# Windowed attention and a squared-ReLU layer on one core: the value products of the later visits by chunk, in quarters of the matmul array

## The chip, the cores and the metric

The kernel runs on one core of a Trainium2 chip. The metric is the device time of one execution in microseconds; a kernel's number is the median of several runs. One execution was profiled besides: its rows are what the prediction reads. A core has five engines that work side by side, each in its own order: TensorE (PE, matmuls), VectorE (DVE), ScalarE (ACT), GpSimd (POOL), and SyncE (SP), which here issues nearly all DMA transfers. PE's rows come in two kinds: PE are the matmuls, PEld the loads of their stationary operand, which lie beside earlier matmuls.

## The reference

```python
for c in range(768 // 32):                       # chunks of 32 queries, 4 batches, 8 heads, 64 wide
    q_c = q[:, :, 32*c : 32*c + 32]
    keys = 8 memory keys + keys from 16 before the chunk to 8 after it
    a = softmax(q_c @ keys.T / 8)
    out[chunk] = a @ values
x = out as 3072 tokens x 512
h = relu(x @ w_in)                               # 512 -> 2048
y = (s * h*h + b) @ w_out                        # 2048 -> 512
```

All is float32. The two large products are done in three matmuls each of a faster 32-bit type, with operands split in a high and a low part.

## The kernel before, in words

The attention is done in blocks of 64 queries (two chunks) against 96 keys: 80 of the block's own window, 16 before and 8 after it counted in, and the rest memory keys with padding. The keys stand in an order such that the first chunk needs keys 0 to 63 and the second keys 32 to 95 (SPANS); the others of the 96 are masked, so that their weights are zero. A visit (attend, L506 on) handles six blocks of a pair of heads, or three blocks of two pairs of heads. There are 32 visits. The first 8 (alone) serve the first 768 tokens; the 24 from the ninth on serve tokens 768 to 1151 (4 visits) and the remaining 1920 tokens (20 visits, whose results go through DRAM, tiles xs, to the later stages).

A visit has these steps. The scores (product, L540): for each of three pairs of blocks and each head four matmuls of 64 x 64 (head width x queries) over 96 keys; a head uses 64 rows of the array, a block 64 of its columns, and the scores of each head of the pair go to a PSUM bank of their own (scs). DVE adds the mask and finds the maximum (L621), ACT takes the exponential and its sum (L625), POOL multiplies by the reciprocal of the sum (L637). The weights are transposed to keys x queries (tile aT): by PE for the first 8 visits, by 32 x 32 blocks on DVE from the ninth on (flip, L654). Then come the values (value, L581): for each block and head one matmul of 96 keys x 64 columns over 64 queries, into a third bank (va, ring "v"). A float32 matmul of the program is two matmul records and two weight loads in the trace, so the 12 value matmuls of a visit are 24 records, and the 12 score matmuls 24 records as well. ACT copies the sums out (L590 for the 20 visits that go through DRAM; L600, with a subtraction on DVE at L601, for the others).

From the ninth visit on the values of a visit are held back by DEPTH = 2 visits and issued by PE as one operation with the scores of the visit two later:

```python
def both():
    for j in range(last[5] if last else 0):
        last[2](j)          # the held-back visit's values
    for j in range(nj):
        product(j)          # this visit's scores
```

So 22 of the 24 visits have values and scores together, the first two of them scores alone, and at the end two visits' values remain, which are issued by themselves.

The order of all instructions on each engine is fixed beforehand by a planner (Plan.lay, L258): a list scheduler with a hold time per kind of operation (HOLD, SCORES, VALUES), priorities with a table of hand-tuned shifts (NUDGE), and a model of DMA landings. PSUM banks are handed out by the planner too: eight banks, with limits per kind in room (L420): two for scores ("s"), at most three of scores and values together, two for the hidden layer ("h"), three accumulators ("acc"), five for the products of the later stage ("p"). On the chip the engines wait for one another by semaphores, and follow that order.

After the attention of the first 1152 tokens the hidden layer (hidden, L703) and the output product (result, L733) run interleaved; the remaining 1920 tokens use a seven-product scheme on 2 x 2 blocks (seven, L934, and rest, L1056). Weights are made from 64-bit inputs by ACT, DVE and POOL in the first quarter (weight, L666 on).

Of the kernel before, what the change touches and what calls it, by code (L numbers as in the profile page):

```python
# [92 lines left out]
BANKS = 8  # L93
# [31 lines left out]
def places(vis):  # L125
# [7 lines left out]
    for run in runs:  # L133
        for n, i in enumerate(run):
# [20 lines left out]
            low=475, affine_v=475, rec=120, max=178, flip=449, xlow=466, wlow=330, wjoin=602, wsign=601, out=600,  # L155
            small=300, prod=1311, half=656, gsum=1220, gsumv=568, tsumv=1067, one=180, chigh=494, scaled=602, add=480, wide=900, keepp=455, storep=640, addp=590, lowp=568, vsum=1260, ssum=700, shigh=950, slow=1143, tsum=1800, thigh=905, tlow=1068, norm=1121, norm2=1860, wrest=1290, issue=440)
SCORES = {3: 680}
VALUES = {3: 1050}
# [207 lines left out]
def body(ctx: ExitStack, tc: tile.TileContext, qkv, w1, w2, out):  # L366
# [46 lines left out]
    aTs = ring("aT", 2, [KB, 2, GP // 2, 2, QB], F32)  # L413
# [6 lines left out]
    def room(r, kind):  # L420
        n = r.live.get
        if kind == "acc":
            r.free += spare
            spare.clear()
            return n("acc", 0) < NT
        if kind == "w":
            return n("w", 0) < 2
        if kind == "p":
            return n("p", 0) < 5
        if kind == "s0":  # L430
            return True
        few = n("s0", 0) + n("s", 0) + n("v", 0)
        if kind in "sv":
            early = not r.next.get("acc", 0)
            return n(kind, 0) < 2 + early and few < 3 + 2 * early
        return n("h", 0) < 2
# [10 lines left out]
    c_id, c_aT, c_mask, c_s, c_b = (fixed() for _ in range(5))  # L447
    op("ACT", "copy", -100, lambda: nc.scalar.activation(s_sb, ones[:, :1], AF.Exp), (), (c_s[0],))
    op("POOL", "copy", -100, lambda: make_identity(nc, ident), (), (c_id[0],))
    def constants():  # L450
        for x in aTs.tiles:
            nc.gpsimd.memset(x, 0.0)

# [14 lines left out]
    op("POOL", "wrest", 5, constants, (), (c_aT[0],))  # L468
# [37 lines left out]
    def attend(vis):  # L506
# [42 lines left out]
        if alone:  # L549
            for j in range(nj):  # L550
                op("PE", "scores", a, lambda j=j: product(j), (piece(j),), (sc(0, j)[j], sc(1, j)[j]))
        else:

            last = open_.pop(0) if len(open_) >= DEPTH else None

            def both():
                for j in range(last[5] if last else 0):
                    last[2](j)
                for j in range(nj):
                    product(j)  # L560

            op("PE", (VALUES[last[5]] if last else 0) + SCORES[nj], a, both, [raw[0], *(last[0] if last else ())],
               [x[j] for x in scs for j in range(nj)] + (last[1] if last else []))
            if last:
                last[3]()
# [5 lines left out]
        if not early:  # L571
            norm(a + 0.5, slice(0, 2), t, st, nj)
            flip(a + 0.5, t, aT, nj)

        va = Val(ps, "v")
# [5 lines left out]
        def value(j):  # L581
            for u in range(2):
                i = 2 * j + u
                for n in range(2):
                    nc.tensor.matmul(av()[n * D:(n + 1) * D, i * QB:(i + 1) * QB],  # L585
                                     v.tile[:KB, (n * nb + i) * D:(n * nb + i + 1) * D], aT.tile[:, n, j, u, :], start=True, stop=True)

        def store():
            if ch is None:
                op("ACT", "xhigh", due + late, lambda: nc.scalar.activation(x.tile[:, :tok], av(), AF.Copy), (va[0],), (x[0],))  # L590
# [5 lines left out]
                op("SP", "issue", due + late, lambda: nc.sync.dma_start(  # L596
                    xs[key][:, i:i + len(cs), lo:lo + n], x.tile[:, :tok].rearrange("q (c t) -> q c t", c=len(cs))), (x[0],),
                   (c_xs[key][vis],), size=P * tok * 4)
                return
            op("ACT", "xhigh", due + late, lambda: nc.scalar.activation(x.tile[c][:, 0], av(), AF.Copy), (va[0],), (x["H", c],))  # L600
            op("DVE", "xlow", due + late, lambda: nc.vector.tensor_tensor(x.tile[c][:, 1], av(), x.tile[c][:, 0].bitcast(F32), ALU.subtract),  # L601
               (va[0], x["H", c]), (x["L", c],))

        def values():
            for j in range(nj):
                op("PE", "value", due + late, lambda j=j: value(j), reads, (va[0],))
            store()

        reads = [v[0]] + list(aT.parts.values())
        if alone:  # L610
            values()
        else:
            open_.append((reads, [va[0]], value, store, values, nj))
# [27 lines left out]
    def turn(a, n, t, aT, act, nj):  # L641
# [5 lines left out]
        ready = [tp[j] for j in range(nj)] + [c_aT[0]]  # L647
        to = lambda: aT.tile[:, n, :nj].rearrange("k j u q -> k j (u q)")
# [5 lines left out]
    def flip(a, t, aT, nj):  # L654

        def block(u, c, g):
            rows, gg = slice(u * QB + c * CHUNK, u * QB + (c + 1) * CHUNK), slice(g * CHUNK, (g + 1) * CHUNK)
            nc.vector.transpose(aT.tile[gg, :, :nj, u, c * CHUNK:(c + 1) * CHUNK], t.tile[rows, :, :nj, gg])  # L658

        for u in range(2):  # L660
            for c in range(NQC):
                for g in range(SPANS[c][0] // CHUNK, SPANS[c][1] // CHUNK):
                    op("DVE", FLIP[nj], a + 0.3, lambda u=u, c=c, g=g: block(u, c, g), [t[n, j] for n in range(2) for j in range(nj)] + [c_aT[0]], (aT[u, c, g],))
# [32 lines left out]
    def hidden(u):  # L696
# [3 lines left out]

        def products(c):
# [4 lines left out]
        for c in range(NC_T):  # L706
            o = op("PE", "hidden", u, lambda c=c: products(c), (x["H", c], x["L", c], w["H"], w["L"]), (h[0],))
# [133 lines left out]
    def old(slot):  # L841
# [4 lines left out]
        return [x_vals[slot[1]][a, c] for a in "HL" for c in range(NC_T)]  # L846
# [265 lines left out]
    while open_:  # L1112
        open_.pop(0)[4]()
# [67 lines left out]
```

## Time and profile before

| | |
|---|---|
| median of 3 runs | 576.74 us (576.28 to 578.23) |
| time of the profiled execution | 578.52 us |
| its span, first to last instruction | 576.7 us |
| PE busy | 565.7 us (98%) |
| DVE, ACT, POOL busy | 430.3, 393.0, 197.6 us |
| matmuls of the values, all 32 visits (L585) | 768 records |
| matmuls of the scores, all 32 visits (L546) | 768 records |

A time in a row is in us unless it says ns. A mean of matmul records (such as 226 ns) is the time from issue to end of one of them; several are under way at once, so that the pace of a group is read from the chain of waits, where a piece stands with the time that it added. There the values of a visit and its scores stand as separate pieces.

### The profile page before, as it was taken

To read this page: it belongs to the slowest core of one execution; us is meant where nothing else is said; L and a number is where in the kernel's file an instruction comes from. 1 tells how busy PE (TensorE), PEld (TensorE's weight loads), DVE (VectorE), ACT (ScalarE), POOL (GpSimd) and SP (SyncE) were. 2 spreads that over 40 slices of the span, in tenths; PEclk is the share of its full clock that TensorE was granted. 3 is DMA by queue.
4 is the path that set the end of the run, shared out by engine and by line. 5 is a ranking of instruction groups with operands and counts; after the bars stand their busy time and mean duration, and the time that the engine had idled before them with its cause. 6 is when DMAs were issued, how large, how long until landed. Compare 5 with 4: busy or idle time off the path is not lost.

```text
span 576.7 us, 11446 instructions
## 1 busy us (share of the span) xinstructions
PE 565.7 (98%) x3950; PEld 482.2 (84%) x3954; DVE 430.3 (75%) x1117; ACT 393.0 (68%) x950; POOL 197.6 (34%) x230
## 2 busy tenths in 40 slices
PE   7989999999999999999999999999999999999997
PEld 4668898898888888898888888888888888888885
DVE  4999889457977887789888677998954544499653
ACT  5999999767877576777676677556726464655552
POOL 4466435876775683216742121000000111100000
PEclk9999999999999999999999999999999999999999
DMA  8956665679999998957999686577876565656661
GB/s 287 408 220 229 235 220 179 213 264 296 337 353 331 337 322 248 352 179 255 286 312 380 216 295 226 200 235 255 292 256 211 190 212 190 212 192 205 232 209 68
DMA packets 70489, 146.20 MB, mean 254 GB/s; under 512 B 6176, under 2 KB 42912, under 8 KB 70432
## 3 DMA queue, kind: packets, MB, share of 16 engines
q1 hardware_dynamic: 70288, 145.36, 75.3%
q8 instruction: 31, 0.51, 0.4%
q14 instruction: 26, 0.21, 0.1%
q10 hardware_dynamic: 144, 0.12, 0.1%
HBM read 105.87 MB, written 39.58 MB: 252 GB/s over the span
## 4 chain that ended last, share of the span: by engine, by line
PE 86%; POOL 4%; ACT 3%; DVE 2%; issue 2%; DMA 2%; SPq 0%; DVEq 0%; POOLq 0%; ACTq 0%
PE ps L1056 26%; PE ps L934 26%; PE ps L733 14%; PE ps L703 13%; PE ps L585 3%; PE ps L546 3%; POOL words L800 2%; POOL words L792 1%; ACT t L625 1%; DMA raw<-qkv 1%; DMA early<-qkv 1%; PE ps L646 1%; ACT ps L676 1%; POOL t L637 1%; ACT w L685 1%
## 5 line engine op out<-in xcount | busy, mean ns | idle before, releaser
L934 PE MATMUL ps<-again,again 128*128 128x480 f32 x672 | 148.3, 381 | 0.0
L934 PEld LDWEIGHTS ps<-again,again 128*128 128x128 f32 x672 | 125.6, 188 | 20.9
L703 PE MATMUL ps<-x,w 128*128 128x384 f32 x576 | 111.4, 339 | 1.2 <-DVE wv L681 0.6
L703 PEld LDWEIGHTS ps<-x,w 128*128 128x128 f32 x576 | 100.6, 188 | 6.9 <-POOL w L688 0.7
L733 PE MATMUL ps<-w,gH 128*128 128x512 f32 x288 | 90.3, 395 | 0.5 <-POOL w L688 0.5
L1056 PE MATMUL ps<-gH,again 128*128 128x482 f32 x272 | 81.5, 380 | 0.0
L625 ACT ACTIVATE t<-t,nmax 128x96 f32<-128x96 f32 x192 | 69.9, 368 | 13.3 <-DVE nmax L621 13.2
L658 DVE STREAM_TRANSPOSE aT<-t 32x192 f32<-32x192 f32 x192 | 70.6, 368 | 9.1 <-POOL t L637 5.8
L733 PEld LDWEIGHTS ps<-w,gH 128*128 128x128 f32 x288 | 54.0, 188 | 11.1 <-POOL w L688 0.8
L1056 PE MATMUL ps<-again,again 128*128 128x482 f32 x264 | 61.8, 382 | 0.0
L733 PE MATMUL ps<-w,gL 128*128 128x512 f32 x144 | 58.4, 405 | 0.3 <-DVE gL L720 0.3
L1056 PEld LDWEIGHTS ps<-gH,again 128*128 128x128 f32 x272 | 51.3, 188 | 8.2
L1056 PEld LDWEIGHTS ps<-again,again 128*128 128x128 f32 x264 | 49.8, 188 | 8.1
L1056 PE MATMUL ps<-gL,again 128*128 128x482 f32 x136 | 51.9, 382 | 0.0
L800 POOL TENSOR_TENSOR words<-words 128x256 f32<-128x256 f32 x64 | 48.2, 752 | 10.0 <-DVE words L804 4.9
L792 POOL TENSOR_TENSOR words<-w 128x512 f32<-128x512 f32 x32 | 42.3, 1336 | 23.5 <-DVE words L887 11.6
L688 POOL TENSOR_TENSOR w<-wv,w 128x512 fp32r<-128x512 f32 x28 | 36.2, 1302 | 30.8 <-ACT w L685 13.3
L621 DVE CUSTOM_DVE_ANT_0 t<-ps,mask 128x96 f32<-128x96 f32 x192 | 37.8, 252 | 10.0 <-PE ps L546 9.5
L637 POOL TENSOR_TENSOR t<-t,rden 128x576 f32<-128x576 f32 (+1 forms) x40 | 38.2, 960 | 19.2 <-DVE rden L636 10.9
L720 DVE TENSOR_TENSOR gL<-ps,gH 128x384 fp32r<-128x384 f32 x48 | 26.5, 553 | 18.3 <-ACT gH L719 18.0
L1044 DVE TENSOR_TENSOR gL<-again,gH 128x480 fp32r<-128x480 f32 x43 | 30.2, 712 | 10.3 <-ACT gH L1043 9.8
L969 POOL TENSOR_TENSOR againx<-againx 128x480 f32<-128x480 f32 x4 | 4.9, 1231 | 95.9 <-ACT againx L968 95.9
(105 smaller groups left out, 894.7 us busy)
## 6 DMA issues: line engine op xcount, KB each, us to landing
again<-w1s SPq DMA_DIRECT2D x56, 512.0 KB, 4.4
again<-w2s SPq DMA_DIRECT2D x56, 512.0 KB, 4.2
words<-w SPq DMA_DIRECT2D x24, 512.0 KB, 4.4
v<-qkv SPq DMA_DIRECT2D x28, 384.0 KB, 5.5
raw<-qkv SPq DMA_DIRECT2D x24, 420.0 KB, 5.3
w1s<-w SPq DMA_DIRECT2D x24, 256.0 KB, 4.3
w1s<-words SPq DMA_DIRECT2D x24, 256.0 KB, 3.9
w2s<-w SPq DMA_DIRECT2D x24, 256.0 KB, 5.2
```

Source lines behind the costliest of these rows:

```text
L621: op("DVE", "max", a + 0.1, lambda j=j: nc.vector.tensor_tensor_reduce(t.tile[:, n, j, :], scv(j), mask[:, kinds[j]], -SCALE, 3.0e38, ALU. ...
L625: op("ACT", "exp", a + 0.2, lambda j=j: nc.scalar.activation(t.tile[:, n, j, :], t.tile[:, n, j, :], AF.Exp, bias=nmax()[:, j:j + 1], scal ...
L637: op("POOL", NORM[len(each)], a + 0.25, lambda: nc.gpsimd.tensor_tensor(t.tile[:, heads, :nj], t.tile[:, heads, :nj], rden().unsqueeze(3). ...
L658: nc.vector.transpose(aT.tile[gg, :, :nj, u, c * CHUNK:(c + 1) * CHUNK], t.tile[rows, :, :nj, gg])
L688: op(low, "vsum" if turn_ else "wjoin", due, lambda: e.tensor_tensor(dst(1), v.tile, dst(0).bitcast(F32), ALU.subtract), (v[0], w["H"]), ( ...
L703: nc.tensor.matmul(h.tile[:, :TOK], weight_tile(0, f)[:, wi, c * P:(c + 1) * P], x.tile[c][:, xi], start=(c == 0 and n == 0), stop=(c == N ...
L733: nc.tensor.matmul(acc.tile, g.tile[gi][:, t * P:(t + 1) * P], weight_tile(1, f)[:, wi, :], start=(first and n == 0), stop=(last and n == 2))
L792: o = op("POOL", "vsum", due, lambda k=k, f=f: nc.gpsimd.tensor_tensor(at(sums, 2 * k, 2), weight_tile(side, f)[:, 0].bitcast(F32), weight ...
L800: op("POOL", "ssum", due, lambda to=to, a=a, b=b, how=how: nc.gpsimd.tensor_tensor(at(sums, to), at(sums, a), at(sums, b), how), [sums[x] ...
L934: nc.tensor.matmul(bank.tile[:, :PT], w.tile[:, lo:lo + P], xv.tile[xi][:, kc], start=(not more and kc == 0 and i == 0), stop=(kc == 1 and ...
L1044: op("DVE", "lowp", due - AHEAD, lambda cut=cut, v=v: nc.vector.tensor_tensor(cut.tile[1][:, :PT], at(v), cut.tile[0][:, :PT].bitcast(F32) ...
L1056: nc.tensor.matmul(sx(bank), w.tile[:, lo:lo + P], cut.tile[xi], start=(first and k == 0), stop=(last and k == 2), skip_group_check=True)
```

## The change

The values from the ninth visit on are computed by chunk: for each block, each half r of the array's rows and each head there is one matmul of 64 keys x 64 columns over the 32 queries of chunk r. The keys that a chunk doesn't need are no longer in its product. A quarter of the array (64 rows, 64 columns) is named by r and the head. There are 24 such matmuls in a visit (48 records) for the 12 before.

- The value tile holds rows 0 to 63 and rows 32 to 95 of the values, one below the other, on all 128 partitions (kernel, the host's layout); the DMA has 128 partitions before and after. aT has 128 partitions: flip writes a chunk's weights into the half of its keys. The memsets of aT on POOL are gone, since no masked part is read any more.
- The sums have no bank of their own: chunk r's go into columns 288 to 479 of the bank in which the scores of head r of the visit two later stand (to). ACT copies them out in two operations of 192 columns, each of which waits for the readers of that bank's scores (L621); for tokens 768 to 1151 DVE subtracts in two operations too.
- room lets the later stage have 6 banks ("p") and the hidden layer 3 after the first 8 visits' values.
- VALUES is 700 for 1050, new holds for the new operations, and NUDGE is another table, so that the planner lays another order of the whole program.

```diff
 NUDGE = {
...
-BANKS = 8
+BANKS, PBANKS = 8, 6
...
-VALUES = {3: 1050}
+VALUES = {3: 700}
...
-    aTs = ring("aT", 2, [KB, 2, GP // 2, 2, QB], F32)
+    aTs = ring("aT", 2, [P, 2, GP // 2, 2, QB], F32)
...
         if kind == "p":
-            return n("p", 0) < 5
+            return n("p", 0) < PBANKS
...
-        return n("h", 0) < 2
+        return n("h", 0) < 2 + (r.next.get("v", 0) >= 3 * NALONE * (H // 2))
...
-    def constants():
-        for x in aTs.tiles:
-            nc.gpsimd.memset(x, 0.0)
...
             def both():
-                for j in range(last[5] if last else 0):
-                    last[2](j)
+                for j in range(last[4] if last else 0):
+                    last[1](j, to)
                 for j in range(nj):
                     product(j)
...
+            to = lambda r: scs[r].tile[:, nj * KB:nj * KB + last[4] * QB]
...
+        def halves(j, out):
+            for u in range(2):
+                i = 2 * j + u
+                for r in range(2):
+                    rows = slice(r * D, (r + 1) * D)
+                    for n in range(2):
+                        nc.tensor.matmul(out(r)[n * D:(n + 1) * D, i * CHUNK:(i + 1) * CHUNK], v.tile[rows, (n * nb + i) * D:(n * nb + i + 1) * D],
+                                         aT.tile[rows, n, j, u, :CHUNK], start=True, stop=True)
...
+            for r in range(NQC):
+                dst = (lambda r=r: split(x.tile[:, :tok])[:, :, r]) if ch is None else (lambda r=r: split(x.tile[c][:, 0])[:, :, r])
+                op("ACT", "xhalf", due_, lambda r=r, dst=dst: nc.scalar.activation(dst(), flat(out(r)), AF.Copy), (),
+                   (*parts[r], x[r] if ch is None else x["H", c, r]))
...
+            for r in range(NQC):
+                op("DVE", "xpart", due_, lambda r=r: nc.vector.tensor_tensor(
+                    split(x.tile[c][:, 1])[:, :, r], flat(out(r)), split(x.tile[c][:, 0])[:, :, r].bitcast(F32), ALU.subtract),
+                   (x["H", c, r],), (*parts[r], x["L", c, r]))
...
-            rows, gg = slice(u * QB + c * CHUNK, u * QB + (c + 1) * CHUNK), slice(g * CHUNK, (g + 1) * CHUNK)
-            nc.vector.transpose(aT.tile[gg, :, :nj, u, c * CHUNK:(c + 1) * CHUNK], t.tile[rows, :, :nj, gg])
+            rows, keys = slice(u * QB + c * CHUNK, u * QB + (c + 1) * CHUNK), slice(g * CHUNK, (g + 1) * CHUNK)
+            lo = c * D + (g - c) * CHUNK
+            nc.vector.transpose(aT.tile[lo:lo + CHUNK, :, :nj, u, :CHUNK], t.tile[rows, :, :nj, keys])
...
+            views[i, :, AT_V:] = np.concatenate([v[lo:hi] for lo, hi in SPANS])
```

## Rows read from the trace of the kernel before

**Rows 1.** The page, span and part 1: busy time, share, instructions.
```profile
span 576.7 us, 11446 instructions
PE 565.7 (98%) x3950; PEld 482.2 (84%) x3954; DVE 430.3 (75%) x1117; ACT 393.0 (68%) x950; POOL 197.6 (34%) x230
```

**Rows 2.** Busy time by stretch: length, then busy (count) of each engine, clock.
```profile
28.00:72.00 44.00, 41.58 (x328) 35.42 (x329) 39.68 (x104) 42.45 (x111) 24.62 (x27) 1.00 0.66 232
...
268.00:350.00 82.00, 82.00 (x620) 69.27 (x618) 66.61 (x189) 56.03 (x141) 31.90 (x36) 1.00 0.90 296
```

**Rows 3.** PE's waits: total us, times, longest.
```profile
PE ps L546 <- DMA early<-qkv: 2.7, 3, 1.3
PE ps L646 <- POOL t L637: 0.9, 1, 0.9
...
PE ps L703 <- DVE wv L681: 0.6, 1, 0.6
PE ps L703 <- POOL w L688: 0.5, 1, 0.5
PE ps L733 <- POOL w L688: 0.5, 1, 0.5
PE ps L733 <- DVE gL L720: 0.3, 1, 0.3
```

**Rows 4.** Chain in order of time, a visit with both: start, us, what.
```profile
225.47 2.10 PE ps L703 x12
227.57 0.85 PE ps L585 x24
228.42 0.66 PE ps L546 x24
229.07 2.28 PE ps L733 x9
...
235.14 2.08 PE ps L733 x9
```

**Rows 5.** The same chain, a visit of scores alone.
```profile
91.41 0.66 PE ps L546 x24
92.06 2.30 PE ps L733 x9
```

**Rows 6.** The same chain, the last two visits' values.
```profile
389.84 1.55 PE ps L585 x48
```

**Rows 7.** Lines L585 and L546: duration ns min/median/max, first and last start.
```profile
L585 PEld LDWEIGHTS ps<-aT,v x672: 132/138/138, 29.1 to 391.1; 96*64 96x64 f32 x168
L585 PE MATMUL ps<-aT,v x672: 222/222/271, 29.1 to 391.2; 96*64 96x64 f32 x168
...
L546 PE MATMUL ps<-raw x672: 242/243/294, 18.3 to 350.0; 64*64 64x96 f32 x168
```

**Rows 8.** Groups by line, weight loads of 128 columns: busy, mean ns, idle.
```profile
L703 PEld LDWEIGHTS ps<-x,w 128*128 128x128 f32 x576 | 100.6, 188 | 6.9 <-POOL w L688 0.7 <-ACT gH L719 0.7 <-DVE w L688 0.4
```

**Rows 9.** Timeline of weight loads at the head of a score group.
```profile
228.34 0.15 PEld L546 LDWEIGHTS ps<-raw 64*64 64x64 f32 x4
```

**Rows 10.** Groups by line and shape: copies and subtractions on ACT and DVE.
```profile
L590 ACT ACTIVATE wv<-ps 128x384 f32<-128x384 f32 x20 | 9.7, 484 | 7.3 <-PE ps L585 7.3
...
L601 DVE TENSOR_TENSOR x<-ps,x 128x384 fp32r<-128x384 f32 x12 | 6.6, 547 | 0.5 <-ACT x L600 0.5
...
L1050 ACT ACTIVATE gH<-const-bfloat16-1.0 128x2 fp32r<-128x2 bf16 x3 | 0.6, 190 | 0.0
...
L1019 DVE SCALAR_TENSOR_TENSOR partial<-ps,s_sb,wv 128x240 f32<-128x240 f32 x2 | 0.8, 463 | 1.9 <-PE ps L1056 1.9
```

**Rows 11.** Timeline of POOL, the memsets of aT.
```profile
1.24 1.41 POOL L452 MEMSET aT<- 96x768 f32 x2
```

**Rows 12.** Timeline: last maximum of a visit, and the next visit's scores.
```profile
230.02 0.25 DVE L621 CUSTOM_DVE_ANT_0 t<-ps,mask 128x96 f32<-128x96 f32 x1
...
232.13 0.73 PE L546 MATMUL ps<-raw 64*64 64x96 f32 x24
```

More of the change, by code (lines that the diff above doesn't have):

```diff
@@ L154 @@
             relu=400, square=400, affine=560, high=371, xhigh=371, wscale=557, whigh=520, copy=270, exp=360, keep=371, store=480, bias=500,
-            low=475, affine_v=475, rec=120, max=178, flip=449, xlow=466, wlow=330, wjoin=602, wsign=601, out=600,
+            low=475, affine_v=475, xhalf=235, xpart=275, rec=120, max=178, flip=449, xlow=466, wlow=330, wjoin=602, wsign=601, out=600,
             small=300, prod=1311, half=656, gsum=1220, gsumv=568, tsumv=1067, one=180, chigh=494, scaled=602, add=480, wide=900, keepp=455, storep=640, addp=590, lowp=568, vsum=1260, ssum=700, shigh=950, slow=1143, tsum=1800, thigh=905, tlow=1068, norm=1121, norm2=1860, wrest=1290, issue=440)
 SCORES = {3: 680}
-VALUES = {3: 1050}
+VALUES = {3: 700}
 NORM = {3: 650, 6: 1109}
@@ L444, in warm @@
         nc.tensor.matmul(idle, ones[:, :P], ones, start=True, stop=True)
-    c_id, c_aT, c_mask, c_s, c_b = (fixed() for _ in range(5))
+    c_id, c_mask, c_s, c_b = (fixed() for _ in range(4))
     op("ACT", "copy", -100, lambda: nc.scalar.activation(s_sb, ones[:, :1], AF.Exp), (), (c_s[0],))
     op("POOL", "copy", -100, lambda: make_identity(nc, ident), (), (c_id[0],))
-    def constants():
-        for x in aTs.tiles:
-            nc.gpsimd.memset(x, 0.0)
     def make_mask():
@@ L467, in body @@
     op("DVE", "wrest", -99, make_mask, (), (c_mask[0],))
-    op("POOL", "wrest", 5, constants, (), (c_aT[0],))
     c_early, c_w = [fixed() for _ in range(NEARLY)], {x[1:]: fixed() for x in ORDER}
@@ L556, in both @@
             def both():
-                for j in range(last[5] if last else 0):
-                    last[2](j)
+                for j in range(last[4] if last else 0):
+                    last[1](j, to)
                 for j in range(nj):
                     product(j)
[L562 to L565, printed above, removed]
+            to = lambda r: scs[r].tile[:, nj * KB:nj * KB + last[4] * QB]
+            op("PE", (VALUES[last[4]] if last else 0) + SCORES[nj], a, both, [raw[0], *(last[0] if last else ())],
+               [x[j] for x in scs for j in range(nj)])
         for n in range(2):
@@ L573, in attend @@
             flip(a + 0.5, t, aT, nj)
-        va = Val(ps, "v")
+            if last:
+                last[2]([[x[j] for j in range(nj)] for x in scs], to)
+        va = Val(ps, "v") if alone else None
         if c == 0 and ch is not None:
@@ L585, in value, with store @@
                     nc.tensor.matmul(av()[n * D:(n + 1) * D, i * QB:(i + 1) * QB],
-                                     v.tile[:KB, (n * nb + i) * D:(n * nb + i + 1) * D], aT.tile[:, n, j, u, :], start=True, stop=True)
-        def store():
+                                     v.tile[:KB, (n * nb + i) * D:(n * nb + i + 1) * D], aT.tile[:KB, n, j, u, :], start=True, stop=True)
+        def halves(j, out):
[6 more added lines that the diff above has]
+                                         aT.tile[rows, n, j, u, :CHUNK], start=True, stop=True)
+        def store(parts, out):
+            due_ = due + late
+            split = lambda x: x.rearrange("p (i r q) -> p i r q", i=nb, r=NQC)
+            flat = lambda x: x.rearrange("p (i q) -> p i q", i=nb)
+            for r in range(NQC):
+                dst = (lambda r=r: split(x.tile[:, :tok])[:, :, r]) if ch is None else (lambda r=r: split(x.tile[c][:, 0])[:, :, r])
+                op("ACT", "xhalf", due_, lambda r=r, dst=dst: nc.scalar.activation(dst(), flat(out(r)), AF.Copy), (),
+                   (*parts[r], x[r] if ch is None else x["H", c, r]))
             if ch is None:
-                op("ACT", "xhigh", due + late, lambda: nc.scalar.activation(x.tile[:, :tok], av(), AF.Copy), (va[0],), (x[0],))
                 cs, gg = [list(dict.fromkeys(k[i] for k in combos)) for i in range(2)]
@@ L595, in store @@
                 staged[key].append((lo, lo + n, vis))
-                op("SP", "issue", due + late, lambda: nc.sync.dma_start(
-                    xs[key][:, i:i + len(cs), lo:lo + n], x.tile[:, :tok].rearrange("q (c t) -> q c t", c=len(cs))), (x[0],),
+                op("SP", "issue", due_, lambda: nc.sync.dma_start(
+                    xs[key][:, i:i + len(cs), lo:lo + n], x.tile[:, :tok].rearrange("q (c t) -> q c t", c=len(cs))), (x[0], x[1]),
                    (c_xs[key][vis],), size=P * tok * 4)
                 return
-            op("ACT", "xhigh", due + late, lambda: nc.scalar.activation(x.tile[c][:, 0], av(), AF.Copy), (va[0],), (x["H", c],))
-            op("DVE", "xlow", due + late, lambda: nc.vector.tensor_tensor(x.tile[c][:, 1], av(), x.tile[c][:, 0].bitcast(F32), ALU.subtract),
-               (va[0], x["H", c]), (x["L", c],))
+            for r in range(NQC):
+                op("DVE", "xpart", due_, lambda r=r: nc.vector.tensor_tensor(
+                    split(x.tile[c][:, 1])[:, :, r], flat(out(r)), split(x.tile[c][:, 0])[:, :, r].bitcast(F32), ALU.subtract),
+                   (x["H", c, r],), (*parts[r], x["L", c, r]))
         def values():
+            outs_ = [Val(ps, "v") for _ in range(NQC)]
+            to = lambda r: outs_[r].tile[:, :nb * CHUNK]
             for j in range(nj):
-                op("PE", "value", due + late, lambda j=j: value(j), reads, (va[0],))
-            store()
+                op("PE", "value", due + late, lambda j=j: halves(j, to), reads, [o[0] for o in outs_])
+            store([[o[0]] for o in outs_], to)
         reads = [v[0]] + list(aT.parts.values())
[L610 to L613, printed above, removed]
+        if not alone:
+            open_.append((reads, halves, store, values, nj))
+            return
+        for j in range(nj):
+            op("PE", "value", due + late, lambda j=j: value(j), reads, (va[0],))
+        op("ACT", "xhigh", due + late, lambda: nc.scalar.activation(x.tile[c][:, 0], av(), AF.Copy), (va[0],), (x["H", c],))
+        op("DVE", "xlow", due + late, lambda: nc.vector.tensor_tensor(x.tile[c][:, 1], av(), x.tile[c][:, 0].bitcast(F32), ALU.subtract),
+           (va[0], x["H", c]), (x["L", c],))
     def weights(a, kinds, n, sc, t, st, scv):
@@ L646, in turn @@
             op("PE", "turn", a + 0.3, lambda j=j: nc.tensor.transpose(keep()[:, j, :], t.tile[:, n, j, :], ident), (t[n, j], c_id[0]), (tp[j],))
-        ready = [tp[j] for j in range(nj)] + [c_aT[0]]
-        to = lambda: aT.tile[:, n, :nj].rearrange("k j u q -> k j (u q)")
+        ready = [tp[j] for j in range(nj)]
+        to = lambda: aT.tile[:KB, n, :nj].rearrange("k j u q -> k j (u q)")
         if act:
@@ L662, in flip @@
                 for g in range(SPANS[c][0] // CHUNK, SPANS[c][1] // CHUNK):
-                    op("DVE", FLIP[nj], a + 0.3, lambda u=u, c=c, g=g: block(u, c, g), [t[n, j] for n in range(2) for j in range(nj)] + [c_aT[0]], (aT[u, c, g],))
+                    op("DVE", FLIP[nj], a + 0.3, lambda u=u, c=c, g=g: block(u, c, g), [t[n, j] for n in range(2) for j in range(nj)], (aT[u, c, g],))
     def weight(i, half, f, due):
@@ L699, in hidden, with inputs @@
         x, w = x_vals[ch], c_w[0, f]
+        def inputs(c):
+            return [x[a, c, *r] for a in "HL" for r in ([()] if ch < NALONE else [(0,), (1,)])]
         def products(c):
@@ L706, in hidden @@
         for c in range(NC_T):
-            o = op("PE", "hidden", u, lambda c=c: products(c), (x["H", c], x["L", c], w["H"], w["L"]), (h[0],))
+            o = op("PE", "hidden", u, lambda c=c: products(c), (*inputs(c), w["H"], w["L"]), (h[0],))
         g = g_vals[u] = Val(gs)
@@ L845, in old @@
             return [g_vals[u][a] for u in range(len(STEPS) - 3, len(STEPS)) for a in "HL"]
-        return [x_vals[slot[1]][a, c] for a in "HL" for c in range(NC_T)]
+        return list(x_vals[slot[1]].parts.values())
     seven_slots = [[(0, b), (1, b)] for b in range(7)]
@@ L1112, in body @@
     while open_:
-        open_.pop(0)[4]()
+        open_.pop(0)[3]()
     for p in range(NPAIR):
@@ L1161 @@
         views[i, :, ends[-1]:ends[-1] + 2] = sb
-        views[i, :KB, AT_V:] = np.stack([vb[g, c] for c, g in combos], axis=2).reshape(KB, 2 * len(combos) * D)
+        v = np.stack([vb[g, c] for c, g in combos], axis=2).reshape(KB, 2 * len(combos) * D)
+        if i < NALONE * (H // 2):
+            views[i, :KB, AT_V:] = v
+        else:
+            views[i, :, AT_V:] = np.concatenate([v[lo:hi] for lo, hi in SPANS])
     arrays = {
```

51 rows, old and new, of the table NUDGE are left out of this document.

## The prediction

> **What bounds the kernel now.** First the page, for whether one engine fills the span: PE is busy 98% of 576.7 us, the next engine 75% [rows 1]. That share is a mean, so the busy times by stretch come next: from 28 to 72 us PE misses 2.4 us of 44, from 268 to 350 nothing of 82, and ACT, the busiest of the others, has 56 of these 82 [rows 2]. What could be won from waits stands in the list of PE's waits: 2.7 us for the first DMAs, then 2.8 us in five waits, 0.9 the longest [rows 3]. So from about 28 us on PE's own work sets the end, and a change counts by what it takes off PE's order, or by a wait that it puts in. The cost of a visit on PE is read from the chain in order of time. With both parts it adds 0.85 for values, 0.66 for scores, and 0.20 to the nine result matmuls behind it (2.28 for 2.08): 1.71 us [rows 4]. With scores alone it is 0.66 and 0.22 [rows 5].
>
> **What a group of values costs.** The two visits left at the end stand in one run of 48 records: 1.55 us [rows 6]. One visit's 24 are 0.85, so 24 more without a break are 0.70, and a break in the array's shape costs 0.15. The 0.70 are 12 pairs (two heads, two column halves side by side) at 58 ns a pair. Is that pace set by the 64 columns streamed, which the change halves, or by the load of 64 weight columns, which it keeps? The rows speak for the load. The first matmul of a group takes 271 ns where the others take 222, and 294 for 242 among the scores: with nothing before it in the new shape it waits some 50 ns for its weights [rows 7]. A load of 128 columns lasts 188 ns, one of 64 columns 138: 50 ns for 64 columns again [rows 7, 8]. Four such loads for four quarters lie beside one another, 0.15 us for all [rows 9], so quarters don't lengthen it.
>
> **The change, part by part.**
>
> 1. Value matmuls, 22 visits. 24 records in 12 pairs become 48 records in 12 sets of four. If the weights set the pace, a set takes the 58 ns of a pair and the matmuls themselves bring nothing: 12 x 58 = 0.70 for 0.70. Bounds: half the streaming, 29 ns a set, is 0.35; records that can't follow faster than the scores' 0.66 / 24 = 27.5 ns are 48 x 27.5 = 1.32 [rows 4]. I take 0.70, since the load of 64 columns is the row nearest to it.
>
> 2. The seam. Values used the array by 96 rows x 64 columns, scores by 64 x 64; now both are 64 x 64. Of three changes of shape in a visit (into the values, into the scores, back to 128 x 128) one goes. Its price from the values is the 0.15 above. From the scores: six sets of four, 96 columns each, at most 58 x 96 / 64 = 87 ns, are 0.52 of their 0.66, which leaves 0.14 [rows 4, 6]. 22 x 0.15 = 3.3 us, all of it in PE's order. The bounds with part 1: -0.35 - 0.15 = -0.50 and +0.62 - 0.15 = +0.47 us a visit.
>
> 3. The last two visits' values stay by themselves and are 24 sets either way: nothing, from -0.7 to +1.2 by the bounds of part 1. The two visits with scores alone and the first eight are as before.
>
> 4. ACT. One copy of 384 columns (484 ns) becomes two of 192. Between 190 ns at 2 columns and 484 at 384 the line gives 336 each, so +0.19 us in 24 visits, 4.5 us. DVE: for four visits, two subtractions between 463 ns (240 columns) and somewhat less in place of one of 547: at most +0.38 each, 1.5 us [rows 10]. Both lie beside PE; ACT has 26 us free in 268 to 350 [rows 2]. Without that cover 4.5 us would be the price.
>
> 5. The wait that is added. Each copy waits for the maxima that read its bank, and the bank comes back only after it. Queued behind it on ACT are the exponentials of the same visit and the hidden layer's steps; PE's next scores wait for the bank. At the closest pair of visits the last maximum starts at 230.02 and the next scores at 232.13 [rows 12]: 2.1 us, in which 0.25 and two copies of 0.34 fit with 1.2 over. Zero is taken; the bounds are nothing and 0.7 a visit (both copies uncovered), 15 us.
>
> 6. Banks. A sixth bank for the products and a third for the hidden layer let PE run ahead, where it waits for nothing in 268 to 350 and for 2.8 us in all after the start [rows 2, 3]: zero, at most 2.8 won.
>
> 7. The memsets on POOL, 1.41 us at 1.24 [rows 11], are over before the first scores' DMA wait of PE ends, and nobody waits for them: zero. The value DMAs have the same 128 partitions and bytes.
>
> 8. The order. Every instruction may move, so the waits of rows 3 can be others. I take them as many as now, and 2.8 us either way: all of those after the start gone, or as many again.
>
> The sum: the profiled execution took 578.52 us with 576.7 of span; minus 3.3 is 575.2 with 573.4 of span. It stands 1.8 above the median, so against the median of 576.74 the same 3.3 give 573.4 us.
>
> **A rule weighed.** Records of the scores start four in a set of at most 87 ns, 22 ns apart in the mean [rows 4, 6]. The Trainium skill, "TensorE: Matmul & The Clock Gate", section "Wait — 56ns, not 53.3ns?", has a floor of about 25 ns from one matmul's start to the next however few its columns; this trace is already a little under that in the scores, so the floor does not hold across quarters here, but no row shows 15 ns in the mean, which the sum needs. By that rule 48 records would be 1.2 us (an estimate from that page). The page "TensorEngine Tiling (Array Packing)", section "Overview", promises up to twice the pace for each small dimension that is packed; by it the values would halve.
>
> **The rivals.**
>
> A. The streaming sets the pace. For it: a pair's 58 ns and 64 columns would fit as well by proportion, scores with 96 columns run at up to 87. Against it: the 50 ns of every load. Then 24 visits win 0.35 more each, 8.4 us: 576.74 - 3.3 - 8.4 = 565.0 us.
>
> B. The issue of records sets the pace. 96 instructions in 0.70 us are more than any row shows: the scores have 48 in 0.66. At the scores' mean start, 22 ns, 48 records are 1.06, +0.36 a visit; minus the seam +0.21, in 22 visits 4.6, and 2 x 0.36 at the end: 582 us, and 588 at 27.5 ns. It is slower from 0.85 / 48 = 17.7 ns a record on.
>
> C. The bank held longer stops PE, on the other side as well. In place of a third bank that PE could fill while ACT emptied it, scores and sums share two, and ACT is strictly in order: a copy behind a 0.48 us step of another kind gives the bank back that much late. For it: before, ACT stood idle for 7.3 us in all until the sums were there [rows 10], so that it often copied them at once; in another order other work may stand ahead. Against: 1.2 us over at the closest pair. With 0.3 us a visit it is 22 x 0.3 - 3.3 = +3.3, 580 us; from 0.15 a visit the gain is gone.
>
> D. The new order gives back what the seam wins, or the seam stays for a reason that no row shows (the change doesn't do what it says): 3 us of waits more, 576.5 us.
>
> **How the numbers follow.** Forecast 0.57, its own range 570.5 to 575.8 (the 2.8 us of part 8). A 0.12, D 0.16, C 0.08, B 0.07. A measurement of this kernel can tell about 0.3% (1.7 us) from no change. Faster than 575.0: nine tenths of the forecast, A and a little of D, 0.65. Within 575.0 to 578.5: the rest of the forecast and most of D, 0.20. Slower: B, C, 0.15. Going out from 573.4, 567.0 to 578.5 leaves out B, half of A and of C, and the forecast's far ends: 0.07 + 0.06 + 0.04 + 0.03 = 0.20.
>
> **What would show it.** Values of 48 records in 12 sets with 0.70 to 0.85 us on the chain, followed by scores of about 0.52 without a break, 1.56 a visit for 1.71; first matmuls of the scores no longer 50 ns longer than the rest; PE's busy time down by about 3 us and its waits after 28 us still below 4. Values at 0.4 would show A, above 0.9 B; waits of PE on ACT's copies ahead of scores would show C; PE's waits grown by 3 us D. If a visit still costs 1.71, the seam was not where the 0.15 is, and the prediction is wrong at its core.

## The result, and the profile after

The changed kernel takes 572.46 us (median of 4 runs, 571.24 to 573.1) against 576.95 for the kernel before in the same runs: a ratio of 0.992, 95% interval 0.989 to 0.994. That is 4.5 us less; 3.3 were forecast. The profiled execution took 572.16 us with 570.4 of span.

The page, span and part 1 of the changed kernel:

```profile
span 570.4 us, 12626 instructions
PE 561.1 (98%) x4525; PEld 480.5 (84%) x4529; DVE 428.0 (75%) x1121; ACT 394.3 (69%) x974; POOL 193.0 (34%) x228
```

PE's busy time is 4.6 us less than in [rows 1], with 575 matmul records more. The 576 that the 24 visits add are there (a record can be missing from a trace). The chain in order of time shows a visit with both parts, and the last two visits' values, which now stand apart:

```profile
204.97 2.08 PE ps L725 x12
207.05 0.83 PE ps L589 x48
207.88 0.53 PE ps L540 x24
208.41 2.28 PE ps L755 x9
...
391.72 0.83 PE ps L589 x48
392.55 5.44 PE ps L1078 x24
398.00 0.83 PE ps L589 x48
398.83 20.59 PE ps L1078 x93
```

L589 are the values, L540 the scores. Values 0.83 for 0.85, scores 0.53 for 0.66, and as before 0.20 in the matmuls behind them: 1.56 us a visit for the 1.71 of [rows 4]. The gain stands in the scores' row, though their matmuls are untouched. That the scores no longer have to bring the array into a new shape is what the experiments below test. The lines of the two groups (duration ns min/median/max) and the first record of one score group on the timeline:

```profile
L589 PEld LDWEIGHTS ps<-aT,v x1152: 129/135/135, 127.7 to 398.6; 64*64 64x64 f32 x192
L589 PE MATMUL ps<-aT,v x1152: 219/219/240, 127.7 to 398.6; 64*64 64x32 f32 x192
```

```profile
158.20 0.27 PE L540 MATMUL ps<-raw 64*64 64x96 f32 x1
```

A value matmul over 32 columns lasts 219 ns, hardly less than the 222 over 64 in [rows 7], and its weight load 135 ns for 138. PE's waits have become fewer than in [rows 3]: after the first 28 us two are left, 0.9 us in place of 2.8.

```profile
...
PE ps L755 <- POOL w L707: 0.7, 1, 0.7
...
PE ps L755 <- DVE rden L654: 0.2, 1, 0.2
```

The rows on ACT and DVE that answer to [rows 10], groups by line and shape:

```profile
L599 ACT ACTIVATE wv<-ps 128x192 f32<-128x192 f32 x40 | 11.6, 317 | 1.6 <-PE ps L589 0.9 <-DVE nmax L639 0.7
...
L612 DVE TENSOR_TENSOR x<-ps,x 128x192 fp32r<-128x192 f32 x8 | 2.6, 347 | 0.4 <-ACT x L599 0.4
```

### The profile page after: what moved, and what is told of

Read it like the earlier page. It is cut to its first block, busy times and chain, and to the rows that moved or that the text cites. A ratio compares the mean times of both kernels' runs of the same rounds, so it can differ in the third digit from the quotient of the medians.

```text
span 570.4 us, 12626 instructions
## 1 busy us (share of the span) xinstructions
PE 561.1 (98%) x4525; PEld 480.5 (84%) x4529; DVE 428.0 (75%) x1121; ACT 394.3 (69%) x974; POOL 193.0 (34%) x228
## 4 chain that ended last, share of the span: by engine, by line
PE 94%; DVE 2%; ACT 1%; DMA 1%; issue 0%; SPq 0%; POOL 0%; DVEq 0%; ACTq 0%
PE ps L1078 26%; PE ps L956 26%; PE ps L755 18%; PE ps L725 17%; PE ps L589 3%; PE ps L540 3%; DMA early<-qkv 1%; PE ps L580 1%; ACT t L643 1%; PE ps L664 0%; DVE t L639 0%; SPq L526 0%; DVE ps L698 0%; DVE wv L700 0%; PE ps L443 0%
## 5 line engine op out<-in xcount | busy, mean ns | idle before, releaser
L652 POOL TENSOR_SCALAR rden<-den 128x6 f32<-128x6 f32 (+1 forms) x40 | 10.7, 268 | 84.8 <-ACT t L643 83.3
```

## The experiments

The first four ask what sets the pace of the value matmuls and where the seam's price lies.

**The kernel before, values and scores in turns.**

```diff
-                for j in range(last[5] if last else 0):
-                    last[2](j)
                 for j in range(nj):
+                    if last:
+                        last[2](j)
                     product(j)
```

> The kernel before, with values and scores of a visit taken in turns by pair of blocks (values 0, scores 0, values 1, ...), in one operation as before, so the planned order is the same. Theory (a break in the array's shape, 96 x 64 against 64 x 64, costs about 0.15 us): four breaks more in each of 22 visits, 88 x 0.15 = 13.2 us, about 590.2 us. Rival (the 0.15 belongs to the operation's semaphores or to the first use of new tiles, not to the shape): within 1 us of 576.9.

Measured: 591.05 us against 576.53 for the kernel before, ratio 1.024 (1.021 to 1.027): 14.5 us for 88 breaks more, 0.165 each. One visit on the chain, the first of its three like pairs of pieces:

```profile
231.73 0.38 PE ps L585 x8
232.12 0.33 PE ps L546 x8
...
```

Three pieces of 0.38 are 1.14 for values that took 0.85 in one piece, and three of 0.33 are 0.99 for 0.66. The matmuls are the same and still one operation; what is added is the change between values and scores. That it is the change of shape, 96 x 64 to 64 x 64, and not the change of kind, the next run shows.

**The changed kernel, in turns as well.** The same edit in the new code.

> The same turns in the changed kernel, where values and scores have one shape. Theory: no break of shape inside a visit; of the 30 ns that the first scores after values take longer, up to 4 more per visit, 88 x 0.03 = 2.6 us at most: 572.5 to 575.1 us. Rival (every change between two kinds of matmul costs 0.15, whatever the shape): 572.5 + 13.2 = 585.7 us.

Measured: 572.8 us, ratio to before 0.992 (0.990 to 0.995), as the changed kernel. One visit, the first two of three pairs:

```profile
223.05 0.36 PE ps L589 x16
223.41 0.20 PE ps L540 x8
223.61 0.20 PE ps L589 x16
223.81 0.19 PE ps L540 x8
...
```

Only the first piece pays for the way in (0.36 for 0.20). With one shape, no cost of changing between the two kinds can be measured; the 2.6 us allowed for were not there.

**Each value matmul over 64 columns.** The diff shows the matmul alone; the run also widens the place of the sums by 32 columns and clears, at the start on POOL, the columns of aT that nothing writes.

```diff
...
-                        nc.tensor.matmul(out(r)[n * D:(n + 1) * D, i * CHUNK:(i + 1) * CHUNK], v.tile[rows, (n * nb + i) * D:(n * nb + i + 1) * D],
-                                         aT.tile[rows, n, j, u, :CHUNK], start=True, stop=True)
+                        nc.tensor.matmul(out(r)[n * D:(n + 1) * D, i * CHUNK:i * CHUNK + QB], v.tile[rows, (n * nb + i) * D:(n * nb + i + 1) * D],
+                                         aT.tile[rows, n, j, u, :], start=True, stop=True)
...
```

> The changed kernel with each value matmul over 64 columns in place of 32 (the 32 more are written over by the next matmul or not read; the output is as before). Same weight loads, same records. Theory (the load of 64 weight columns sets the pace, 58 ns a set): sets stay at 58 to 60 ns, 572.5 us within 1.5. Rival (streaming sets the pace, or the change's matmuls are faster for their 32 columns): up to +27 ns in each of 24 x 12 sets, +7.7 us, 580.2 us.

Measured: 572.58 us, ratio 0.992 (0.990 to 0.995).

**Each over 16.** The same place with `:16` and `i * CHUNK + 16`.

> The changed kernel with each value matmul over the first 16 of the chunk's 32 queries (the sums of the other 16 are left out). Theory (weight load sets the pace): 572.5 us within 1, sets of 58 to 59 ns. Rival (streaming sets it): 24 x 12 sets shorter by up to 13 ns, -3.8 us, 568.7 us.

Measured: 572.8 us, ratio 0.992 (0.989 to 0.995). The chain's two pieces of a visit with 64 columns, then with 16:

```profile
311.93 0.86 PE ps L594 x48
312.79 0.50 PE ps L545 x24
```

```profile
223.42 0.82 PE ps L589 x48
224.24 0.54 PE ps L540 x24
```

1.36 us for both in either, 1.36 with 32 columns too. From 16 to 64 columns streamed the set's pace does not move: it is not the streaming, and rival A is out. What all three share is the load of 64 weight columns, but also the 48 records; the last run but one, with 24 records, bears on those.

The next four ask what the order is worth, which was given nothing but a margin.

**The changed code with the plan's numbers of before.**

```diff
 NUDGE = {
...
-BANKS, PBANKS = 8, 6
+BANKS, PBANKS = 8, 5
...
-VALUES = {3: 700}
+VALUES = {3: 1050}
...
-        return n("h", 0) < 2 + (r.next.get("v", 0) >= 3 * NALONE * (H // 2))
+        return n("h", 0) < 2
```

> The changed code with the planner's table, its 1050 for the values and its bank limits as before the change. Theory (the seam is 22 x 0.16 = 3.5 us of the gain, the new order the remaining 0.5 to 1): about 573.0 us, between 572.5 and 574.5. Rival (the new order is the larger part): 575 us or more.

Measured: 584.01 us, ratio 1.011 (1.010 to 1.013). On the rival's side of 575 us, but beyond what it meant: slower than the kernel before, although the seam is gone. PE's largest wait:

```profile
PE ps L957 <- DVE again L906: 3.6, 2, 3.2
```

L906 makes operands of the products that follow the attention (L957), and here PE waits for them at their first stage. A likely reason is that the old table puts them late when the operations around them have other lengths; the run does not separate the table from the bank limits and the hold.

**The kernel before with the new table.** NUDGE alone is exchanged.

> The kernel before with the new table alone. Theory (a table fits the program for which it was made): between 576 and 579 us, no gain. Rival (the new table is worth some 1 us by itself, in the first 40 us): 575.5 us.

Measured: 606.59 us, ratio 1.051 (1.048 to 1.053): far above the theory's 576 to 579, and the rival's 575.5 failed too. PE's largest wait is of the same kind:

```profile
PE ps L933 <- DVE again L882: 10.9, 3, 7.7
```

**The changed kernel with the bank limits of before.** The two bank edits of the run before the last, and no other.

> The changed kernel with 5 banks for the later stage's products and 2 for the hidden layer, as before the change. Theory (PE waited for no bank): 572.5 us within 1. Rival (the sixth and the third bank are what took PE's waits after 28 us from 2.8 to 0.9 us): 574.4 us or more.

Measured: 616.83 us, ratio 1.067 (1.065 to 1.069). The theory failed; it is the rival's direction, at more than twenty times its size (44 us above the theory's 572.5, where the rival had 1.9). It does not show what a bank is worth: the limits change the plan, the last values end at 447.6 for 398.8 us, and PE waited for what hangs on them. PE's rows of the last values and of the first two products of the second stage, and the end of the chain ahead of the second product:

```profile
446.36 1.28 PE L589 MATMUL ps<-aT,v 64*64 64x32 f32 x36 [0.49 <-DVE aT L677]
457.28 2.77 PE L956 MATMUL ps<-again,again 128*128 128x480 f32 x6 [9.64 <-DVE again L905]
463.65 8.67 PE L956 MATMUL ps<-again,again 128*128 128x480 f32 x26 [3.60 <-DVE again L905]
```

```profile
449.96 5.29 DMA xs<-wv
455.26 3.88 DMA words<-xs
459.23 2.23 DVE words L909 x2
461.45 2.15 DVE again L905 x2
```

From the last values' end (446.36 + 1.28) through DRAM and back (5.3 and 3.9 us of transfers) to DVE's operand and the stage's second product, at 463.65, 16 us pass.

**The last two visits' values in one run.** PE's priority for them is set to one value, and for these two visits the bank limits are raised.

```diff
...
+            both_due = 79.5
...
-                op("PE", "value", due + late, lambda j=j: halves(j, to), reads, [o[0] for o in outs_])
+                op("PE", "value", both_due, lambda j=j: halves(j, to), reads, [o[0] for o in outs_])
...
-            return n(kind, 0) < 2 + early and few < 3 + 2 * early
+            end = kind == "v" and r.next.get("v", 0) >= 3 * NALONE * (H // 2)
+            return n(kind, 0) < 2 + early + 2 * end and few < 3 + 2 * early + 3 * end
```

> The changed kernel with the last two visits' values brought together on PE, in one run of 96 records. Theory: one way into 64 x 64 and back is saved, 0.14 + 0.20 us; on the chain one piece of about 1.53 us for two of 0.83, and 572.2 us, which timing can't tell from 572.5. Rival (the later first half delays the second pair's transforms): PE waits at the second stage of products, over 573.

Measured: 581.62 us, ratio 1.007 (1.006 to 1.009). The rival, and larger. PE's row of the values, then of the first three products of the second stage (six matmuls each; the last row holds the third product and what follows):

```profile
405.43 1.60 PE L590 MATMUL ps<-aT,v 64*64 64x32 f32 x96
...
420.22 1.48 PE L958 MATMUL ps<-again,again 128*128 128x480 f32 x6
422.36 1.56 PE L958 MATMUL ps<-again,again 128*128 128x480 f32 x6 [0.66 <-ACT wv L968]
429.00 5.25 PE L958 MATMUL ps<-again,again 128*128 128x480 f32 x15 [5.08 <-DVE again L907]
```

The values are one run of 1.60 us, as the theory had it. But PE stood still for 5 us ahead of the third product. The chain to it, and the copies of the second visit on ACT:

```profile
406.94 3.77 DMA xs<-wv
...
412.00 6.26 DMA xs<-wv
...
418.32 6.17 DMA words<-xs
...
424.59 2.23 DVE words L911 x2
426.81 2.15 DVE again L907 x2
```

```profile
410.79 0.55 ACT L600 ACTIVATE wv<-ps 128x192 f32<-128x192 f32 x2 [0.31 <-DMA xs<-wv]
```

The last values end at 407.0 (405.43 + 1.60), 8.2 us later than the changed kernel's 398.83. The second visit's copies come 4.4 us after the first's (406.36); the end of that is a wait for the first visit's transfer. From the last values to the third product 22.0 us pass. The changed kernel runs its second stage without a wait:

```profile
419.26 21.10 PE L956 MATMUL ps<-again,again 128*128 128x480 f32 x96
```

At 21.10 / 96 = 0.22 a matmul its third product starts at 421.9, so that the start came 7.1 us later here. The rest of the 9.0 us between the two spans (579.4 and 570.4) is mostly the clock. Busy times by stretch (length, PE, PEld, DVE, ACT, POOL, granted clock, DMA):

```profile
424.00:429.00 5.00, 0.00 (x0) 0.00 (x0) 4.41 (x5) 3.01 (x3) 0.00 (x0) 0.69 0.39 152
429.00:433.00 4.00, 4.00 (x11) 3.35 (x11) 3.28 (x4) 1.46 (x2) 0.00 (x0) 0.53 0.09 15
```

After 5 us without a matmul PE works from 429 to 433 near the lower of its two levels (0.53 of full speed; the levels are 1.2 and 2.4 GHz). The 10 or 11 matmuls of these 4 us would have taken 2.2 to 2.4 at 0.22 each: 1.6 to 1.8 us on top of the later start, 8.7 to 8.9 of the 9.0.

Plans thus differ by as much as tens of microseconds, and only a run with the very same order can price the shape.

**The old shape in the new order.** The diff shows the matmuls alone; the copies, the subtractions and the transposes on DVE keep their number and sizes and are fitted to where the sums and weights now stand, and aT is cleared once at the start on POOL.

```diff
...
-                for r in range(2):
-                    rows = slice(r * D, (r + 1) * D)
-                    for n in range(2):
-                        nc.tensor.matmul(out(r)[n * D:(n + 1) * D, i * CHUNK:(i + 1) * CHUNK], v.tile[rows, (n * nb + i) * D:(n * nb + i + 1) * D],
-                                         aT.tile[rows, n, j, u, :CHUNK], start=True, stop=True)
+                for n in range(2):
+                    at = i % nj * QB
+                    nc.tensor.matmul(out(i // nj)[n * D:(n + 1) * D, at:at + QB], v.tile[:, (n * nb + i) * D:(n * nb + i + 1) * D],
+                                     aT.tile[:, n, j, u, :], start=True, stop=True)
...
```

> The changed kernel, every engine's order, banks and copies kept, with the values of the late visits in 12 matmuls of 128 rows x 64 columns over 64 queries for the 24 by quarters (it leaves out clearing the parts of aT that a chunk doesn't need, so those sums are other numbers). This puts the break of shape between values and scores back and nothing else. Theory: 22 x 0.16 = 3.5 us, 576.0 us, values and scores 0.85 + 0.66 on the chain. Rival (the gain is the order's, the shape is worth nothing here): 572.5 us within 1.

Measured: 575.85 us (13 runs), ratio 0.9976 (0.9967 to 0.9986). The changed kernel's is 0.9917, so the shape is worth 0.59%, 3.4 us, give or take 1.5 by the two intervals. The three runs above that keep the changed kernel's order of operations and its shape (0.9919 to 0.9922) give 3.1 to 3.3. It is back on the chain where it was looked for (the shape is 128 x 64 here and not 96 x 64; the pieces are those of [rows 4]):

```profile
299.86 1.10 PE ps L960 x5
300.96 0.85 PE ps L593 x24
301.81 0.66 PE ps L545 x24
```

The run undoes more than the break: it has 24 value records a visit for 48. That they take 0.85 on the chain where the 48 took 0.83 shows that the number of records does not set the pace either, and leaves the difference in the scores' piece, 0.66 for 0.53.

The rest of the gain, 1 - 0.9976 = 0.24% or 1.4 us (0.8 to 1.9 by the interval), is then what order, banks and copies bring. PE's waits after 28 us are 1.2 us here, also without the new shape, for the 2.8 of [rows 3]:

```profile
PE ps L759 <- POOL w L711: 0.7, 1, 0.7
PE ps L960 <- DVE again L909: 0.3, 1, 0.3
PE ps L759 <- DVE rden L658: 0.2, 1, 0.2
```

**The planner told what a visit takes.**

```diff
-VALUES = {3: 700}
+VALUES = {3: 870}
```

> The changed kernel with the planner's hold of the values at 870 ns in place of 700, which with 680 for the scores is the 1.55 us that a visit takes by the trace; the table of shifts stays. Theory (the table was made for a plan and any other plan meets it by chance; the later stages' operands come late): slower, 575 to 610 us, with PE waiting for DVE's operands at the start of a stage of products. Rival (a truer plan is a better plan): 572.5 us or less.

Measured: 578.6 us, ratio 1.003 (1.002 to 1.004), with 3.2 us of waiting for DVE's operands at the first stage, as the theory said. The hold is nearer to the 1.56 us that a visit takes, and the kernel is slower:

```profile
PE ps L956 <- DVE again L905: 3.2, 1, 3.2
```

## Why the prediction was right, and where it was not

**PE's order sets the end.** It held: PE is busy 98% as before, and what the seam took from PE's order came off the time (3.4 of the 4.5 us). In the two profiled executions PE is 4.6 us less busy, 1.3 more than the seam's 3.3; the one before stood 1.8 us above its median, and no run tells where the 1.3 belong.

**Part 1, the matmuls bring nothing.** Right: 16, 32 and 64 columns have one pace, and so have 24 records and 48. That the load of the weights sets the pace is what remains once these two are excluded, and is not shown: no run varied the weight columns. The sign that the prediction leaned on was weaker than it took it: the first matmuls' 50 ns have become 21 (240 for 219) with the same 64 columns to load. One group on the timeline:

```profile
222.62 0.90 PE L589 MATMUL ps<-aT,v 64*64 64x32 f32 x48
```

The last record takes 0.22 of the 0.90 us, so 48 starts lie (0.90 - 0.22) / 47 = 14.5 ns apart in the mean. B, for which the limit was 17.7 ns, is out. The floor of 25 ns that the Trainium skill has in "TensorE: Matmul & The Clock Gate", section "Wait — 56ns, not 53.3ns?", does not hold for four quarters in turn, by the same row.

**Part 2, the seam.** Right in kind and size: 0.15 a visit forecast, 1.71 - 1.56 = 0.15 on the chain, 0.165 for each added break, and 3.4 us for 22 visits (give or take 1.5) when the shape is put back, where 3.3 were forecast.

**What would show it** asked too much in one place: the first score matmuls were to last no longer than the others. They last some 30 ns more (0.27 us for the median 0.243). It may be that values that stream 32 columns are over before the scores' weights are in; in the run with 64 columns streamed the first two score matmuls lasted 0.25 together:

```profile
158.19 0.25 PE L545 MATMUL ps<-raw 64*64 64x96 f32 x2
```

**Part 3, the last values** were taken as one run. They stand apart at 391.72 and 398.00, 0.83 each and about 0.2 in the matmuls behind, some 0.3 us dearer than one run of 1.55. The run that joined them shows why a plan may keep them apart: joined there, they came 8.2 us later, and the second stage had to wait.

**Parts 4 and 5, copies and the wait.** Zero was right, C did not come about: PE waits for no bank in the rows after. A copy of 192 columns took 317 ns (336 estimated), the subtraction 347.

**Parts 6 to 8, banks and order.** The sum took them at zero with 2.8 us either way (573.4 give or take 2.8 is 570.6 to 576.2; the range says 570.5 to 575.8), and this is the step whose size was argued badly. Order, banks and copies brought 1.4 us, inside the 2.8 allowed; this is why the whole gain was 4.5 and not 3.3. In the profiles it is fewer waits of PE after 28 us (0.9 for 2.8, and 1.2 with the old shape in the new order) and, in the windows, 0.88 us missed from 28 to 72 for the 2.4 of [rows 2]; which of the three brought it no run here tells. The row (length, then PE's busy time):

```profile
28.00:72.00 44.00, 43.12 (x360) 37.13 (x359) 41.69 (x111) 44.00 (x121) 25.72 (x28) 1.00 0.74 253
```

The margin, though, came from the waits that one good plan has. Five other plans took 2 to 39 us more than the kernel before, 6 for the changed code under the old numbers, 29 for the old code under the new table. D was priced at 3 us of waits; with a plan not made for the program it can be many times that. The change under the plan of before was slower than the kernel before, so the 3.4 us of the seam depend on a plan made for the change, though they don't come from it. That the waits of the new plan would be no more than the old one's was argued from no row; that they were fewer was, for the forecast, luck.

## What to carry to other kernels

Where groups of small matmuls alternate, read the price of a change of the array's shape from two rows: one group by itself and two without a break. Giving neighbours one shape wins that price even where the matmuls themselves get no faster; and before making them narrower, ask whether the streamed columns set their pace at all. In a kernel whose order is fixed beforehand, price a new order by the longest chain off the busy engine (here sums, DRAM, transforms, 16 and 22 us in two runs) and its slack, not by the waits of the plan at hand.

## What was not expected of the hardware

Four quarters of the array took records 14.5 ns apart in the mean, a pace that no row of before showed, and 16, 32 or 64 streamed columns made no difference to it. And 5 us without a matmul cost more than 5 us: the granted clock was 0.69 in that stretch and 0.53 in the four after it, with PE busy throughout, which cost another 1.6 to 1.8 us.
